# Side work placed head by head in the first pass of an attention and token-mixing kernel

## The chip, the cores and the metric

The kernel runs on one core of a Trainium2 chip. Its time is device microseconds of one execution; a version is run several times and the median counts. A profiled execution gives, beside its own time, a span (from its first to its last instruction) and a record of every engine: TensorE (PE, with its weight loads as PEld), VectorE (DVE), ScalarE (ACT), GpSimd (POOL) and SyncE (SP), which issues nearly all DMAs here from one queue. Each engine works through its own instructions in order.

## The reference

```
h = layernorm(x) * (1 + ca) + sa            # x: 2048 x 1024; the six rows sa ca ga sb cb gb = silu(c) @ w_mod
q, k, v = h @ wq, h @ wk, h @ wv            # 32 heads of 32, four segments of 512 tokens
for s in range(4):                          # per head
    p = softmax(q_s k_s^T * scale + causal mask);  a_dot = p v_s
    a_mem = phi(q_s) M / (phi(q_s) z)       # phi(t) = t + 1 for t > 0, else exp(t)
    out_s = g * a_mem + (1 - g) * a_dot     # g = sigmoid(beta)
    M += phi(k_s)^T v_s;  z += sum phi(k_s)
x = x + ga * (out @ wo)
h = layernorm(x) * (1 + cb) + sb
x = x + gb * mixer(layernorm(h))            # token-mixing MLP: 2048 tokens -> 3584 -> 2048, over 1024 channels
```

All is float32 to the outside. Most matmuls are done as three products of parts: a matrix is split into a high part, rounded to the format that TensorE multiplies at full rate, and the rest ("split": a copy on ScalarE, a subtraction on VectorE or GpSimd).

## The kernel before

There are three stages: a start, in which the first 512 tokens are normalised and modulated (to about 115 us); the attention loop (to about 1080 us); the output projection and the mixer. The change is in the attention loop.

The loop runs over 128 steps n, one per head of an iteration. An iteration t takes one group of four heads and one segment of 512 tokens. The 16 iterations of the first pass cover segments 0 and 1 for the eight groups in turn, the 16 of the second pass segments 2 and 3. So n 0 to 63 is the first pass, n 64 to 127 the second. At step n the loop body writes out, for different heads, the stages of one pipeline: `scores` of head n (L440: score matmuls, exponentials on ScalarE into p, two GpSimd masks at L457, the cast of p to the half-precision ph at L459, the rest of p by two GpSimd subtractions at L461), `maxima` of head n + 3 (L414: matmuls sx, sy, sz and on VectorE the row maxima at L425, which go back into the stacks sk by small DMAs at L437), `values` of head n - 1 (L463: 20 short matmuls pv from ph), and `project` for m = n + 8 (L322: key, value and query matmuls at L185 and L193, and the stacks sk of the head by DMAs L318 to L320).

Beside this main work stands side work:

- Weights of a group. In the first pass `load_part` (L149) loads a raw tile of 512 KB (L154) and splits it into two tiles w at L155 to L158; `keep_w` stores the split weights to DRAM, from where the second pass reloads them. A group has value and key weights in two parts ("v", 0 and 1) and query weights in one ("q").
- Token tiles. `token_tile` (L219) loads 128 tokens of segments 2 and 3 (L222), takes the statistics on VectorE (L128), normalises on ScalarE (L207), transposes on TensorE (L228, tile hpl), modulates on ScalarE (L231), splits (L234, L236) and stores to DRAM (L239). There are eight, at n = 4, 9, ... 39.
- Late modulation. `mod_late` (L498) loads 128 rows of the transposed w_mod (L500) and takes one product with the silu row on VectorE (L501), 32 times, at n = 12, 15, ... 105 (ML0, MLS). After the eighth the rows of ga are written to DRAM, after the last the rest.
- Output weights. `wo_ahead` (L552) loads a piece of wo (L556), multiplies it by ga (tile gaw, GpSimd, L557), splits it (L558, L559) and stores it (L561), eight times, at n = 66, 71, ... 101 (WO0, WOS). `spread` loads gaw at n = 62. The pieces are read back from n = 115 on (wop).

All raw tiles of this side work, the high parts of the token tiles and the wo pieces share one set of three buffers (tag "raw").

The order in which the calls stand is not the order on the engines. A scheduler takes all instructions, by the order of the calls and by when it reckons them ready, and gives each engine its own queue; work that waits for no earlier result, such as a load with a free buffer, can so be pulled far ahead. `tc.issue_after(ins)` adds an edge that keeps what a block contains behind `ins` in the queue of the same engine; it orders issue and waits for nothing.

Of the kernel before, what the change touches and what calls it, by code (L numbers as in the profile page):

```python
# [7 lines left out]
F32 = mybir.dt.float32  # L8
# [26 lines left out]
ML0 = 12  # L35
MLS = 3
HB = 3
WO0 = 66
WOS = 5
# [5 lines left out]
def attention_and_mlp(ctx, tc, x, wq, wkv, wo, beta, w1, b1, w2, b2, c, wm_a, wm_b, out):  # L45
# [26 lines left out]
    acst.tile([P, 24], F32, name="pad2")  # L72
# [75 lines left out]

    def load_part(g, pr, kind, part, res):  # L149


        if pr == 0:
            r = a.tile([P, D], F32, tag="raw", bufs=3, name=f"raw{kind}{g}_{part}")
            SY.dma_start(r, (wkv if kind == "v" else wq)[g, :, 1024 * part:1024 * part + 1024])  # L154
        for i in range(2):  # L155
            w = aw.tile([P, 2, 512], F32R, tag="w", bufs=8, name=f"w{kind}{pr}_{g}_{part}_{i}")
            if pr == 0:
                split(w, r[:, 512 * i:512 * i + 512], A, V)  # L158
            else:
                SY.dma_start(w.bitcast(F32), wsp[g, 2 * part + i if kind == "v" else 4 + i])  # L160
            res[kind, 2 * part + i] = w
# [252 lines left out]
    def maxima(t, h):  # L414
# [8 lines left out]
        for i, o in ((0, x[:, 0:128]), (2, x[:, 128:512]), (1, y[:, 0:256]), (3, z)):  # L423
            T.matmul(o, q[:, 128 * i:128 * i + 128], k[:, 0:128 * i + 128], start=True, stop=True)  # L424
            V.tensor_tensor_reduce(o, o, mask[:, 384 - 128 * i:], 1.0, -3.0e38, op0=ALU.add, op1=ALU.max,  # L425
                                   accum_out=mx[:, h % 2, i:i + 1])
# [12 lines left out]

    def scores(t, h):  # L440
        d = st[t]
        q, k = d["sk", h][:, 0], d["sk", h][:, 1]
# [16 lines left out]
        A.copy(ph[:, 0], p32)  # L459
        for c in (slice(0, 640), slice(640, 1280)):  # L460
            G.tensor_tensor(ph[:, 1, c], p32[:, c], ph[:, 0, c], op=ALU.subtract)  # L461
# [36 lines left out]
    def mod_late(j):  # L498
        r = a.tile([P, D], F32, tag="raw", bufs=3, name=f"rawm{j}")
        SY.dma_start(r, wm_b[P * j:P * j + P])  # L500
        V.scalar_tensor_tensor(r, r, 1.0, scb, op0=ALU.mult, op1=ALU.mult, accum_out=mcol[:, j:j + 1])  # L501
# [50 lines left out]
    def wo_ahead(i):  # L552

        nh, c2 = i // 4, 2 * (i % 4)
        r, hi = (a.tile([P, 2, 512], F32, tag="raw", bufs=3, name=f"wo{n_}{i}") for n_ in ("r", "h"))
        SY.dma_start(r, wo[P * c2:P * c2 + 2 * P, 512 * nh:512 * nh + 512].rearrange("(c p) n -> p c n", p=P))  # L556
        G.tensor_tensor(r, r, gaw[:, 512 * nh:512 * nh + 512].unsqueeze(1).to_broadcast([P, 2, 512]), op=ALU.mult)  # L557
        A.copy(hi.bitcast(F32R), r)  # L558
        V.tensor_tensor(r.bitcast(F32R), r, hi, op=ALU.subtract)  # L559
        for part, t in enumerate((hi, r)):  # L560
            SY.dma_start(wos[c2:c2 + 2, nh, :, part].rearrange("c p n -> p c n"), t)  # L561

    for n in range(-LEADS, 4 * NI + VL):
# [15 lines left out]
        if n == WO0 - 4:  # L579
            spread(gaw, 0)  # L580
        if n >= WO0 and (n - WO0) % WOS == 0 and (n - WO0) // WOS < 8:
            wo_ahead((n - WO0) // WOS)
# [365 lines left out]
```

## Time and profile before

| | |
|---|---|
| median of 3 runs | 2335.71 us (2332.09 to 2339.83) |
| profiled execution, its own time | 2329.09 us |
| span of the profiled execution | 2327.4 us |
| granted TensorE clock, mean over the span | 0.983 |
| chain that ended last, by engine | PE 82%, DMA 6%, DVE 6%, ACT 2%, POOL 2% |
| DMA traffic | 414.67 MB, mean 178 GB/s |

How the views are read: a row of the windows gives, for a stretch of the span, the busy time and the number of instructions of each engine, the clock that TensorE was granted (1.00 is full), the mean busy share of the 16 DMA engines and their rate. A row of the waits gives how long an engine stood idle just before instructions of one line, and what ended the wait. A row of the order of time gives start, duration, engine, line, operation and tiles, with the idle time before it and its releaser in brackets. A row with three durations gives least, median and greatest in ns.

### The profile page before, as it was taken

Reading aid. Unit: us, or ns where it says so; the run is one execution under the profiler, and the core shown is the slowest. Engines: PE = TensorE matmul, PEld = TensorE weight load, DVE = VectorE, ACT = ScalarE, POOL = GpSimd, SP = SyncE. Lnnn points to the kernel's source line nnn. Section 1 sums busy time; section 2 is a strip of 40 time slices with the busy share of each in tenths; the row PEclk is TensorE's granted clock in tenths of the full one; section 3 lists DMA queues with packets and bytes.
Section 4 is the critical chain, followed back from the end, with each engine's and each line's share of the span. In section 5 each row is a group of like instructions: output and inputs, shape, how many; then the busy total and the mean of one; then the engine's idle time right before and its main releaser. Section 6 shows DMA issues by size and latency. Waiting matters only on the chain.

```text
span 2327.4 us, 38419 instructions
## 1 busy us (share of the span) xinstructions
PE 2244.8 (96%) x13866; PEld 1931.2 (83%) x13866; DVE 1693.3 (73%) x3806; ACT 1107.6 (48%) x2010; POOL 721.8 (31%) x827
## 2 busy tenths in 40 slices
PE   8999999999899999998989999999999999999999
PEld 7888888888789999986877888888888788888887
DVE  5666666785776566657889666598889787868687
ACT  5476766655566666655324333353335242424232
POOL 3165555675676555555000000023332000000000
PEclk9999999999999999999999999999999999999999
DMA  6747565788774444374354765465557542423233
GB/s 245 247 122 217 179 185 150 231 295 271 219 218 121 122 119 120 105 238 139 128 195 166 285 227 211 147 251 212 213 213 270 186 136 78 140 69 128 67 116 147
DMA packets 172593, 414.67 MB, mean 178 GB/s; under 512 B 17236, under 2 KB 71540, under 8 KB 163444
## 3 DMA queue, kind: packets, MB, share of 16 engines
q1 hardware_dynamic: 172404, 412.22, 53.3%
q8 instruction: 110, 1.80, 0.3%
q14 instruction: 79, 0.65, 0.1%
HBM read 236.23 MB, written 125.06 MB: 155 GB/s over the span
## 4 chain that ended last, share of the span: by engine, by line
PE 82%; DMA 6%; DVE 6%; ACT 2%; POOL 2%; issue 2%; SPq 1%; DVEq 0%; POOLq 0%; ACTq 0%
PE mx L745 44%; PE nps L185 12%; PE qps L193 7%; PE po L653 6%; PE pv L475 3%; PE sx L424 1%; PE a L446 1%; PE sz L424 1%; DMA rawx<-in_x_dram 1%; DMA rawm<-in_wm_b_dram 1%; PE a L449 1%; DMA wor<-in_wo_dram 1%; PE rd L396 1%; PE a L453 1%; PE up L406 1%
## 5 line engine op out<-in xcount | busy, mean ns | idle before, releaser
L745 PE MATMUL mx<-bU,sp 128*128 128x512 f32 x2352 | 535.6, 389 | 2.6 <-DVE sp L123 1.3
L745 PEld LDWEIGHTS mx<-bU,sp 128*128 128x128 f32 x2352 | 440.9, 188 | 96.8 <-DVE sp L123 2.1
L185 PE MATMUL nps<-wv,h 128*128 128x256 f32 x3072 | 447.6, 287 | 1.3 <-POOL h L123 1.1
L745 PE MATMUL mx<-bA,sp 128*128 128x512 f32 x1764 | 431.7, 389 | 3.4 <-DVE sp L123 1.8
L120 ACT CAST sp<-wr 128x384 fp32r<-128x384 f32 (+2 forms) x408 | 217.3, 545 | 445.5 <-PE mx L745 377.5
L461 POOL TENSOR_TENSOR ph<-p,ph 128x640 f16<-128x640 f32 x256 | 374.5, 1484 | 148.8 <-ACT ph L459 143.4
L185 PEld LDWEIGHTS nps<-wv,h 128*128 128x128 f32 x3072 | 409.8, 192 | 6.3 <-POOL h L123 1.3
L745 PEld LDWEIGHTS mx<-bA,sp 128*128 128x128 f32 x1764 | 330.7, 188 | 73.6 <-DVE sp L123 2.6
L123 DVE TENSOR_TENSOR sp<-wr,sp 128x384 fp32r<-128x384 f32 (+2 forms) x408 | 261.0, 651 | 33.7 <-ACT sp L120 33.2
L752 DVE TENSOR_TENSOR ac<-mx,ac 128x512 f32<-128x512 f32 x280 | 190.4, 689 | 91.0 <-PE mx L745 90.3
L193 PE MATMUL qps<-h,wq 128*128 128x512 f32 x768 | 200.1, 408 | 1.4 <-DVE r L349 1.3
L459 ACT CAST ph<-p 128x1280 f16<-128x1280 f32 x128 | 160.8, 1257 | 69.9 <-POOL p L457 69.3
L653 PE MATMUL po<-wo,ots 128*128 128x512 f32 x768 | 184.0, 398 | 8.1 <-DVE x L656 5.9
L653 PEld LDWEIGHTS po<-wo,ots 128*128 128x128 f32 x768 | 146.5, 192 | 40.1 <-issue 6.7
L193 PEld LDWEIGHTS qps<-h,wq 128*128 128x128 f32 x768 | 147.0, 197 | 31.8 <-issue 1.7
L457 POOL TENSOR_SCALAR_AFFINE_SELECT p<-p 128x256 f32<-128x256 f32 x256 | 126.1, 501 | 138.5 <-ACT p L454 88.4
L475 PE MATMUL pv<-vp,ph 128*128 128x97 bf16 (+1 forms) x2560 | 156.9, 205 | 10.8 <-POOL ph L461 4.5
L425 DVE CUSTOM_DVE_ANT_0 sx<-sx,mask 128x128 f32<-128x128 f32 (+1 forms) x256 | 110.5, 432 | 75.0 <-PE sx L424 73.8
L745 PE MATMUL mx<-bB,sp 128*128 128x512 f32 x588 | 164.5, 389 | 0.0
L475 PEld LDWEIGHTS <-ph 128*128 128x128 f16 x2560 | 121.0, 100 | 40.4 <-issue 17.1
L752 DVE TENSOR_TENSOR cc<-mx,cc 128x512 f32<-128x512 f32 x140 | 94.6, 685 | 53.4 <-PE mx L745 48.4
L745 PEld LDWEIGHTS mx<-bB,sp 128*128 128x128 f32 x588 | 110.3, 188 | 23.3 <-ACT bB L120 0.4
(173 smaller groups left out, 3184.6 us busy)
## 6 DMA issues: line engine op xcount, KB each, us to landing
sk<-sg SPq DMA_DIRECT2D x384, 128.0 KB
wr<-in_w_dram SPq DMA_DIRECT2D x28, 1024.0 KB
wr<-in_w_dram SPq DMA_DIRECT2D x32, 768.0 KB
bstu<-ucd SPq DMA_DIRECT2D x28, 768.0 KB
wsp<-wv SPq DMA_DIRECT2D x32, 512.0 KB
rawm<-in_wm_b_dram SPq DMA_DIRECT2D x32, 512.0 KB
wv<-wsp SPq DMA_DIRECT2D x32, 512.0 KB
pcd<-cc SPq DMA_DIRECT2D x14, 1024.0 KB
```

What stands on the lines that cost most here:

```text
L120: A.copy(hi, src)
L123: lo_eng.tensor_tensor(lo, src, hi.bitcast(F32), op=ALU.subtract)
L185: T.matmul(ps[:, aa], h[:, j, 128 * tt:128 * tt + 128], wt[:, i, o:o + 256], start=(n == 0), stop=(n >= 6 * NK - 2), skip_group_check=True)
L193: T.matmul(ps, wt[:, i, o:o + 128], h[:, j], start=(k + n == 0), stop=(3 * k + n == 3 * NK - 1))
L425: V.tensor_tensor_reduce(o, o, mask[:, 384 - 128 * i:], 1.0, -3.0e38, op0=ALU.add, op1=ALU.max, accum_out=mx[:, h % 2, i:i + 1])
L457: G.affine_select(w, w, pattern=[[0, 2], [1, 128]], compare_op=ALU.is_ge, fill=0.0, base=0, channel_multiplier=-1)
L459: A.copy(ph[:, 0], p32)
L461: G.tensor_tensor(ph[:, 1, c], p32[:, c], ph[:, 0, c], op=ALU.subtract)
L475: T.matmul(pv[:, i, 0:w], ph[:, part, o:o + 128], d["vp"][:, j, h, 0:w], start=(n == 0), stop=(n == 19), skip_group_check=True)
L653: T.matmul(ps, os_[:, i, P * ct:P * ct + P], wop[ct, nh][:, j], start=(n == 0), stop=(n == 3 * NK - 1))
L745: T.matmul(ps, ops[q][:, i, P * k:P * k + P], b[:, j], start=(m == 0 and first), stop=(m == 3 * nk - 1), skip_group_check=True)
L752: V.tensor_tensor(d, ps, d, op=ALU.add)
```

## The change

The calls of the side work are taken out of the loop body and put into a table `todo` by step; each piece of side work is cut into a fetch (its load) and the rest, and the rest is put behind an instruction of that step's own head. `marks` holds, for each step, the last row maximum on VectorE ("V", that of head n + 3), the cast on ScalarE ("A") and the last subtraction on GpSimd ("G").

- Token tiles load into gaw, which is not needed for ga before n = 62, in place of a raw buffer, at n = 0, 5, ... 35, and are worked on two steps later, VectorE's part behind the mark "V".
- The weights of groups 2 to 7 load their parts at steps 0, 1 and 2 after 8g - 13 and are split at steps 1, 3 and 4 after it, ScalarE's part behind the mark "A". Groups 0 and 1 are as before.
- Late modulation j loads at n = 40 + 2j, its product comes at n = 42 + 2j behind the mark "V".
- Output weights i load at n = 65 + 6i, the split comes two steps later, GpSimd's part behind the mark "G"; the piece is multiplied and split in two halves.
- A padding tile is 16 floats smaller, so the mask, the memory, the split weights w and the tiles of the projections and stacks lie 64 bytes lower in each partition. The pages of h, p and ph stay where they were.

```
-ML0 = 12
-MLS = 3
+ML0 = 40
+MLS = 2
-WO0 = 66
-WOS = 5
+WO0 = 65
+WOS = 6
...
-    acst.tile([P, 24], F32, name="pad2")
+    acst.tile([P, 8], F32, name="pad2")
...
+    def fetch_part(g, kind, part):
+        r = a.tile([P, D], F32, tag="raw", bufs=3, name=f"raw{kind}{g}_{part}")
+        SY.dma_start(r, (wkv if kind == "v" else wq)[g, :, 1024 * part:1024 * part + 1024])
+        return r
+
+    def split_part(g, kind, part, r):
+
+        for i in range(2):
+            w = aw.tile([P, 2, 512], F32R, tag="w", bufs=8, name=f"w{kind}0_{g}_{part}_{i}")
+            split(w, r[:, 512 * i:512 * i + 512], A, V)
+            W[0, g][kind, 2 * part + i] = w
...
     def token_tile(tt):
 
-        r = a.tile([P, D], F32, tag="raw", bufs=3, name=f"rawx{tt}")
-        SY.dma_start(r, x[P * tt:P * tt + P])
+        r = gaw
         norm_x(a, r)
...
+    marks = {}
+
+    @contextmanager
+    def behind(n, engines):
+
+        with ExitStack() as s:
+            for e in engines:
+                if (n, e) in marks:
+                    s.enter_context(tc.issue_after(marks[n, e].ins))
+            yield
...
+    def wo_split(i, r):
+
+        nh, c2 = i // 4, 2 * (i % 4)
+        hi = a.tile([P, 2, 512], F32, tag="raw", bufs=3, name=f"woh{i}")
+        for j in range(2):
+            G.tensor_tensor(r[:, j], r[:, j], gaw[:, 512 * nh:512 * nh + 512], op=ALU.mult)
+            A.copy(hi[:, j].bitcast(F32R), r[:, j])
+            V.tensor_tensor(r[:, j].bitcast(F32R), r[:, j], hi[:, j], op=ALU.subtract)
         for part, t in enumerate((hi, r)):
             SY.dma_start(wos[c2:c2 + 2, nh, :, part].rearrange("c p n -> p c n"), t)
+
+    todo = {}
+
+    def plan(n, f, engines=""):
+        todo.setdefault(n, []).append((f, engines))
+
+    def later(n, fetch, m, f, engines):
+
+        got = []
+        plan(n, lambda: got.append(fetch()))
+        plan(m, lambda: f(got[0]), engines)
+
+    for i in range(8):
+        later(5 * i, lambda i=i: SY.dma_start(gaw, x[P * (8 + i):P * (9 + i)]),
+              5 * i + 2, lambda r, i=i: token_tile(8 + i), "V")
+    for g in range(2, NG):
+        n = 8 * g - 13
+        plan(n, lambda g=g: W.__setitem__((0, g), {}))
+        for kind, part, n0, n1 in (("v", 0, 0, 1), ("v", 1, 1, 3), ("q", 0, 2, 4)):
+            later(n + n0, lambda g=g, kind=kind, part=part: fetch_part(g, kind, part),
+                  n + n1, lambda r, g=g, kind=kind, part=part: split_part(g, kind, part, r), "A")
+        plan(n + 4, lambda g=g: keep_w(g))
+    for j in range(32):
+        n = ML0 + MLS * j
+        later(n, lambda j=j: mod_fetch(j), n + 2, lambda r, j=j: mod_late(j, r), "V")
+    plan(WO0 - 3, lambda: spread(gaw, 0))
+    for i in range(8):
+        n = WO0 + WOS * i
+        later(n, lambda i=i: wo_fetch(i), n + 2, lambda r, i=i: wo_split(i, r), "G")
...
-        if 4 <= n < 44 and n % 5 == 4:
-            token_tile(8 + n // 5)
-        if n >= ML0 and (n - ML0) % MLS == 0 and (n - ML0) // MLS < 32:
-            mod_late((n - ML0) // MLS)
+        for f, engines in todo.pop(n, ()):
+            with behind(n, engines):
+                f()
```

More of the change, by code (lines that the diff above doesn't have):

```diff
@@ L1 @@
 import math
-from contextlib import ExitStack
+from contextlib import ExitStack, contextmanager
 import concourse.bass as bass
@@ L147, in attention_and_mlp @@
     raw_w = {}
+    def fetch_part(g, kind, part):
[7 more added lines that the diff above has]
+            W[0, g][kind, 2 * part + i] = w
     def load_part(g, pr, kind, part, res):
         if pr == 0:
-            r = a.tile([P, D], F32, tag="raw", bufs=3, name=f"raw{kind}{g}_{part}")
-            SY.dma_start(r, (wkv if kind == "v" else wq)[g, :, 1024 * part:1024 * part + 1024])
+            split_part(g, kind, part, fetch_part(g, kind, part))
+            return
         for i in range(2):
             w = aw.tile([P, 2, 512], F32R, tag="w", bufs=8, name=f"w{kind}{pr}_{g}_{part}_{i}")
[L157 to L160, printed above, removed]
+            SY.dma_start(w.bitcast(F32), wsp[g, 2 * part + i if kind == "v" else 4 + i])
             res[kind, 2 * part + i] = w
@@ L424, in maxima @@
             T.matmul(o, q[:, 128 * i:128 * i + 128], k[:, 0:128 * i + 128], start=True, stop=True)
-            V.tensor_tensor_reduce(o, o, mask[:, 384 - 128 * i:], 1.0, -3.0e38, op0=ALU.add, op1=ALU.max,
-                                   accum_out=mx[:, h % 2, i:i + 1])
+            marks[4 * t + h - LEADS, "V"] = V.tensor_tensor_reduce(
+                o, o, mask[:, 384 - 128 * i:], 1.0, -3.0e38, op0=ALU.add, op1=ALU.max,
+                accum_out=mx[:, h % 2, i:i + 1])
         if h % 2 == 0:
@@ L578, in attention_and_mlp @@
             reload_h(seg, ct + 1)
[L579 to L582, printed above, removed]
         if 4 * NI - 5 <= m < 4 * NI + 3:
```

17 lines of the change are left out of this document (9 added, 8 removed).

## The prediction

> **What bounds the kernel now.** I read the page first, then a table of three stretches of the attention stage, then the waits of the stretch that turned out to be slow, then the order of time around single stalls. The page says that TensorE is busy nearly all the time:
>
> ```profile
> span 2327.4 us, 38419 instructions
> PE 2244.8 (96%) x13866; PEld 1931.2 (83%) x13866; DVE 1693.3 (73%) x3806; ACT 1107.6 (48%) x2010; POOL 721.8 (31%) x827
> ```
>
> That is an average over stages. The change touches only the loop over the 128 heads (64 of each pass), so I cut that loop by its casts of L459, one for each head. The stretches end where cast 48, cast 72 and cast 112 start; the columns are length, busy time and count of PE, PEld, DVE, ACT, POOL, granted clock, DMA share and rate. The second fence is the same stretches for L459 alone.
>
> ```profile
> core 0: us, PE busy (x) PEld busy (x) DVE busy (x) ACT busy (x) POOL busy (x), PEclk, DMA share, GB/s
> 115.70:492.30 376.60, 354.57 (x2963) 320.07 (x2962) 258.74 (x773) 262.51 (x492) 231.43 (x257) 0.94 0.63 189
> 492.30:693.90 201.60, 185.34 (x1583) 168.60 (x1582) 136.78 (x391) 113.24 (x196) 130.99 (x139) 0.96 0.77 246
> 693.90:975.50 281.60, 280.79 (x2492) 257.98 (x2491) 172.06 (x584) 176.11 (x312) 164.41 (x224) 1.00 0.44 121
> ```
>
> ```profile
> 115.70:492.30 376.60, 60.36 (x48) 0.94 0.63 189
> 492.30:693.90 201.60, 30.21 (x24) 0.96 0.77 246
> 693.90:975.50 281.60, 50.18 (x40) 1.00 0.44 121
> ```
>
> Heads 72 to 111 carry almost no side work. TensorE is never idle there, at full clock: 281.60 / 40 = 7.04 us a head. That is the floor of a head, since an iteration of the first pass does the same matmuls (per two iterations the same reads and updates of the memory). Beside it the first pass has the token tiles' transposes, 0.91 us a tile in the chain that ended last, 8 x 0.91 = 7.3 us:
>
> ```profile
> 219.30 0.91 PE hpl L228 x8
> ```
>
> Heads 0 to 47 take 376.6 - 48 x 7.04 - 7.3 = 31.4 us too long, heads 48 to 71 take 201.6 - 24 x 7.04 = 32.6 us too long: **64 us** that TensorE loses. The same from the other columns: it is idle for 22.0 + 16.3 = 38.3 us, and the clock is 0.06 and 0.04 short, 22.6 + 8.1 = 30.7 us; 69 us less the 7.3 us of transposes is 62. These stretches, and not the 96%, are where side work can win or lose.
>
> Who waits in that stretch (us in total, times, longest):
>
> ```profile
> DVE rawm L501 <- DMA rawm<-in_wm_b_dram: 30.3, 13, 6.8
> ACT wv L120 <- DMA rawv<-in_wkv_dram: 14.4, 6, 5.4
> POOL wor L557 <- DMA wor<-in_wo_dram: 9.4, 4, 5.6
> DVE st L128 <- DMA rawx<-in_x_dram: 3.6, 3, 2.5
> ```
>
> All four are side work at the front of an in-order engine whose load hasn't landed: 57.7 us. How one reaches TensorE:
>
> ```profile
> 626.25 0.58 SPq L500 DMA_DIRECT2D rawm<-in_wm_b_dram  x1
> 631.84 1.23 DVE L501 SCALAR_TENSOR_TENSOR rawm<-rawm,scb 128x1024 f32<-128x1024 f32 x1 [6.79 <-DMA rawm<-in_wm_b_dram]
> 633.80 0.58 PE L424 MATMUL sy<-sk 96*128 96x256 f32 x1 [3.94 <-DVE rdd L398]
> ```
>
> The load is issued at 626.25, VectorE has nothing left that it may do and sits 6.79 us; the row maxima and the memory read stand behind the product, and TensorE runs dry for 3.94 us. The clock then drops. The ten microseconds around this stall and two like it, and the waits at the head of the other two:
>
> ```profile
> 500.00:510.00 10.00, 7.85 (x46) 6.36 (x46) 8.65 (x20) 4.36 (x10) 9.10 (x9) 0.83 0.75 270
> 540.00:550.00 10.00, 7.53 (x55) 7.03 (x54) 6.06 (x20) 5.86 (x11) 5.36 (x3) 0.83 0.96 354
> 630.00:640.00 10.00, 6.20 (x29) 5.25 (x30) 7.53 (x25) 3.54 (x9) 4.42 (x4) 0.66 0.43 160
> ```
>
> ```profile
> 495.13 2.37 POOL L557 TENSOR_TENSOR wor<-wor,gaw 128x1024 f32<-128x1024 f32 x1 [1.64 <-DMA wor<-in_wo_dram]
> 538.89 1.25 DVE L501 SCALAR_TENSOR_TENSOR rawm<-rawm,scb 128x1024 f32<-128x1024 f32 x1 [4.35 <-DMA rawm<-in_wm_b_dram]
> 544.64 2.37 POOL L557 TENSOR_TENSOR wor<-wor,gaw 128x1024 f32<-128x1024 f32 x1 [5.58 <-DMA wor<-in_wo_dram]
> ```
>
> Idle plus missing clock: 2.15 + 1.7, 2.47 + 1.7 and 3.8 + 3.4, together 15.2 us for 1.64 + 4.35 + 5.58 + 6.79 = 18.4 us of waiting, 0.83 us lost for each. Over 57.7 us that makes **48 of the 64 us late loads**; the other 16 I call crowding (0.22 us a head).
>
> The Trainium skill ("TensorE: Matmul & The Clock Gate", Part 1) says that the array falls to half clock after an idle window of about 3.4 us. By that rule only the third of these stalls would have cost clock, and the gain would be the idle part, about 38 us at most; the trace differs, with 0.83 in a stretch whose idle time is 2.15 us in all, so the sum goes by the rows.
>
> **The change part by part.** *Late modulation.* Its 32 products go from every third head from 12 (in the built program of before the scheduler had pulled them as far forward as loads allowed, all done before cast 72) to every second head from 42 to 104, each load two heads ahead and each product behind the row maxima that VectorE then has. The order of the changed program shows exactly that: one product after every second head's maxima, its load on SP at least two heads earlier, 14 us against the 5 to 6 us that passed in the row above. Heads 0 to 41 lose all of it. *Token tiles* (through gaw in place of a raw buffer) load two heads before their statistics; *weights* two heads, in places one, before the splits, which stand behind that head's cast on ScalarE; *wo* pieces load two heads before GpSimd's product, which stands behind that head's subtraction. So the four waits lose their ground. What remains late by a head or less are a few weight loads (the query part of group 6 is issued about one head ahead): I leave 10%, 48 - 5 = 43 us won. Of the crowding in heads 0 to 71 I take half as gone, since the 32 products and all 8 wo pieces are spread over 70 heads in place of some 58: 8 us.
>
> *What comes in.* Durations (ns, min/median/max):
>
> ```profile
> L501 DVE SCALAR_TENSOR_TENSOR rawm<-rawm,scb x32: 1201/1448/3156, 207.6 to 677.5; 128x1024 f32<-128x1024 f32 x32
> L557 POOL TENSOR_TENSOR wor<-wor,gaw x8: 2363/2390/2847, 495.1 to 665.7; 128x1024 f32<-128x1024 f32 x8
> L236 POOL TENSOR_TENSOR rawx<-rawx,hix x16: 1273/1290/2284, 146.0 to 437.5; 128x512 fp32r<-128x512 f32 x16
> L120 ACT CAST wv<-rawv x32: 602/616/645, 16.6 to 460.9; 128x512 fp32r<-128x512 f32 x32
> L123 DVE TENSOR_TENSOR wv<-rawv,wv x32: 661/692/1776, 17.2 to 461.5; 128x512 fp32r<-128x512 f32 x32
> ```
>
> A wo piece in halves costs GpSimd 2 x 1290, ScalarE 2 x 616, VectorE 2 x 692 ns, hence 0.2 us more on GpSimd than one L557 and nothing that TensorE sees. Heads 72 to 111 get 20 products and 7 pieces: VectorE (172.1 + 29.0 + 9.7) / 281.6 = 75%, ScalarE (176.1 + 8.6) / 281.6 = 66%, GpSimd (164.4 + 18.1) / 281.6 = 65%. TensorE stayed full at more than that, in a part of the first pass whose loads were in time:
>
> ```profile
> 270.00:280.00 10.00, 10.00 (x74) 8.45 (x73) 7.77 (x23) 9.50 (x18) 6.26 (x8) 1.00 0.99 336
> ...
> sum 50.00, PE 50.00 PEld 45.76 DVE 38.70 ACT 38.69 POOL 33.33; mean PE 10.00 PEld 9.15 DVE 7.74 ACT 7.74 POOL 6.67
> ```
>
> So this cost lies between 0 and the crowding rate, 41 heads (72 to 112) x 0.22 = 9 us; 50 us are a short witness, I take 9. The pieces' DMAs (each 512 KB in and twice that out, with 512 KB a product) move along and add some 60 GB/s to a stretch at 121. What is late next: the modulation rows for gaw come with product 7 at head 56, and gaw is loaded at 62, six heads or 42 us later; the last wo piece is split behind head 109, the reload begins at 115; the last rows stand at 104, needed after 127. None decides.
>
> *Waits that are added.* The placement orders issues and waits for nothing. But gaw is one buffer, and its next load waits on SP for the store of the tile before; behind it stand that head's stacks (sk). Token tiles are five heads, 35 us, apart, so this is nothing if the tile's chain keeps to its two heads, and otherwise the second rival.
>
> *Weights 64 bytes lower.* No row shows the same matmul at two addresses. The nearest:
>
> ```profile
> L396 PE MATMUL rd<-MZ,pq x192: 273/276/358, 92.2 to 1036.4; 128*128 128x132 f32 x192
> L185 PE MATMUL nps<-wv,h x3072: 276/283/562, 27.0 to 1013.0; 128*128 128x256 f32 x192
> ```
>
> The moving tile of L396 is one of eight that lie 528 bytes apart, so it starts at eight offsets within 128 bytes, and least and median differ by 3 ns. I take nothing; the ends are the 7 ns between the two medians on 3072 matmuls, 21 us either way.
>
> Sum: -43 - 8 + 9 = **-42 us**. The profiled execution took 2329.1 us (span 2327.4), the median of the runs is 2335.7; I take the difference from the median: 2294 us.
>
> **The rivals.**
>
> (a) *The waits move.* The three raw buffers now hold a product's load for over two heads and two buffers of each wo piece, and SP is one queue: a load that waits there for its buffer holds the stacks behind it. For: three buffers for up to four tenants from head 65 on. Against: no piece overlaps in heads 0 to 41, where half of the loss was. Half of the 48 us is won, the 9 paid: -15, 2321 us.
>
> (b) *Slower: the second pass takes the density of heads 48 to 71.* They did 14 products (two instructions each in the row below) and the 8 pieces in 24 heads at 201.6 / 24 = 8.40 us.
>
> ```profile
> 492.30:693.90 201.60, 23.48 (x28) 0.96 0.77 246
> ```
>
> If density sets that pace, and not late loads, heads 72 to 112 pay 41 x 1.36 = 56 us and heads 42 to 71 keep theirs, while heads 0 to 41 win at most 31.4 x 42 / 48 = 27: +29, 2365 us. It turns slower than before from 27 / 41 = 0.66 us a head. Against it: half the density per head, and the 50 us above at full rate. The Trainium skill ("SBUF — State Buffer", Who interferes with whom) speaks for it: a VectorE instruction with two SBUF inputs shuts out a GpSimd instruction that reads SBUF, and the product is one. The trace has products of 1201 to 3156 ns, so something like it is there, though the same 32 ran beside a busier GpSimd before.
>
> (c) *The address decides*: 21 us better, 2273, or worse, 2315.
>
> (d) *It does not do what it says*: TensorE's lost time comes from the chain of each head and not from the loads; the three stalls above speak against it. 2336 us.
>
> **How the numbers follow.** The sum has 0.57 (its own range 2280 to 2310), (a) 0.17, (b) 0.10, (c) 0.06 better and 0.04 worse, (d) 0.06. 0.3%, 7 us, is about what can be told from no change: faster 0.82 (the sum, (c), 0.15 of (a)), within 0.08 ((d) and the rest of (a)), slower 0.10 ((b)). The range 2268 to 2328 takes in both ends of (c), the low end of the sum and (a), and leaves out (b), (d) and a few hundredths below.
>
> **What would show it.** Right: the first 64 casts of L459 take under 475 us in place of 513, the clock in heads 0 to 71 is at least 0.98, the four waits sum to under 12 us, heads 72 to 111 take at most 291 us. Wrong: the waits gone and the pace still over 7.5 us ((d)); waits of SP or of the wo product ((a)); heads 72 to 111 over 300 us with POOL or DVE as TensorE's releaser ((b)); a median of L185 off by 5 ns ((c)).

## The result and the profile after

| | before | after |
|---|---|---|
| median of 4 runs | 2333.90 us (2331.99 to 2339.83) | 2306.51 us (2305.48 to 2307.91) |
| ratio, 95% interval | | 0.988 (0.9865 to 0.9894) |
| profiled execution, its own time | 2329.09 us | 2305.58 us |

The changed kernel is 27 us faster; 42 us were forecast. The first lines of its page:

```profile
span 2303.9 us, 38456 instructions
PE 2232.7 (97%) x13866; PEld 1918.9 (83%) x13866; DVE 1703.9 (74%) x3814; ACT 1105.6 (48%) x2018; POOL 727.9 (32%) x835
```

The cast of each head is L479 now. Cut at the casts of heads 0, 48, 72 and 112, as before:

```profile
core 0: us, PE busy (x) PEld busy (x) DVE busy (x) ACT busy (x) POOL busy (x), PEclk, DMA share, GB/s
112.20:479.90 367.70, 349.86 (x2998) 315.65 (x2997) 250.89 (x742) 262.18 (x494) 222.24 (x258) 0.95 0.60 171
479.90:664.70 184.80, 178.43 (x1541) 162.28 (x1541) 123.33 (x388) 105.99 (x191) 107.20 (x131) 0.97 0.73 227
664.70:952.80 288.10, 280.05 (x2514) 257.74 (x2513) 206.41 (x632) 181.08 (x326) 202.78 (x240) 0.99 0.62 181
```

Heads 0 to 71 take 552.5 us, 25.7 less than before. TensorE's loss there (idle time and missing clock, read off as for before) is 17.8 + 18.4 in the first row and 6.4 + 5.5 in the second: 48 us where it was 69. Heads 72 to 111, which have got the moved work, take 288.1 us, 6.5 more. What lies ahead of the first cast is 3.5 us shorter, what lies behind head 111 0.7 us shorter: together the 23.5 us by which the spans differ.

The same heads cut at head 42 as well, before and then after:

```profile
115.72:454.37 338.65, 319.70 (x2675) 288.31 (x2674) 226.73 (x690) 236.46 (x447) 201.54 (x230) 0.94 0.60 178
454.37:694.02 239.65, 220.31 (x1872) 200.46 (x1872) 168.91 (x475) 139.40 (x242) 160.87 (x166) 0.95 0.79 253
```

```profile
112.18:439.93 327.75, 309.96 (x2612) 278.20 (x2611) 221.53 (x668) 234.41 (x444) 196.63 (x229) 0.95 0.60 173
439.93:664.67 224.74, 218.31 (x1927) 199.71 (x1926) 152.68 (x462) 133.75 (x240) 132.78 (x160) 0.98 0.70 213
```

In these traces the clock is half for whole steps of 3.41 us, and each such step costs 1.71 us. With the steps counted (11 and 7 before, 10 and 3 after) in place of the two-digit mean, TensorE's loss falls from 37.7 to 34.9 us in heads 0 to 41 and from 31.3 to 11.5 us in heads 42 to 71. So nearly all of it was won in heads 42 to 71. The lengths alone say less, since the stretches do not hold quite the same work: 2675 and 1872 matmuls before, 2612 and 1927 after.

The waits in heads 0 to 71, of which the four that summed to 57.7 us were the ground of the forecast:

```profile
SPq L513 <- ACT ot L512: 52.8, 11, 12.7
SPq L604 <- DMA hT<-gaw: 11.5, 5, 4.5
PE kps L363 <- DVE r L356: 6.8, 3, 4.1
PE a L466 <- DMA sk<-nt: 3.2, 2, 1.8
DVE st L128 <- DMA gaw<-in_x_dram: 2.5, 1, 2.5
DVE rawm L524 <- DMA rawm<-in_wm_b_dram: 0.5, 1, 0.5
```

Of the late loads 3.0 us are left: the first step of the forecast came true. But 48 us of TensorE's loss stayed without them, and there are waits that were smaller or absent before: SP behind the stores of a head (L513) and behind the one buffer of the token tiles (L604), and TensorE behind the small copies sk<-nt. The same two rows of SP and TensorE before, the first in heads 0 to 71, the second in heads 0 to 111:

```profile
SPq L493 <- ACT ot L492: 26.8, 8, 10.0
```

```profile
PE a L446 <- DMA sk<-nt: 0.4, 1, 0.4
```

Over heads 0 to 111 the second is 8.2 us after. Two of these stalls in the order of time, the first with the stretch of half clock around it:

```profile
132.44 0.37 SPq L246 DMA_DIRECT2D hT<-gaw  x1
...
135.94 0.35 SPq L604 DMA_DIRECT2D gaw<-in_x_dram  x1
...
141.77 0.69 DVE L128 BATCH_NORM_STATS2 st<-gaw 128x6 f32<-128x512 f32 x1 [2.51 <-DMA gaw<-in_x_dram]
...
143.31 0.90 PE L363 MATMUL kps<-ident,k 128*128 128x128 f32 x3 [4.09 <-DVE r L356]
```

```profile
131.00:148.10 17.10, 11.28 (x48) 8.18 (x47) 10.87 (x30) 11.50 (x20) 12.48 (x16) 0.50 0.66 187
```

The store of one token tile is issued at 132.44; the load of the next into the same buffer goes out at 135.94 only; VectorE stands for 2.51 us at the statistics, and the remainder r, for which TensorE waits, stands behind them. It is the placed work with its load late after all, by the single buffer. The half clock began at 131.03, before this stall, and behind a step of 3.41 us in which TensorE was idle for 0.1 us only; what began it is open. The second, in the second pass:

```profile
779.54 0.58 SPq L520 DMA_DIRECT2D rawm<-in_wm_b_dram  x1
780.16 0.45 SPq L578 DMA_DIRECT2D wor<-in_wo_dram  x1
780.71 0.41 SPq L520 DMA_DIRECT2D rawm<-in_wm_b_dram  x1
781.22 2.63 SPq L445 DMA_DIRECT2D sk<-nt  x4
786.41 0.77 PE L466 MATMUL a<-sk 98*128 98x512 f32 x1 [2.83 <-DMA sk<-nt]
```

Three loads of 512 KB are issued just ahead of the four copies of 2 KB that a head's scores need, and TensorE waits 2.83 us for these.

The other expectations: the first 64 casts take 494.8 us (112.2 to 607.0), not under 475; heads 72 to 111 stay under 291; the clock of heads 0 to 71 is 0.95 and 0.97 in the two rows, not 0.98; the median of the key and value matmuls fell by 5 ns, as in the third rival, and that of the query matmuls rose by 5. The rows of after, and between them the query matmuls of before:

```profile
L193 PE MATMUL nps<-wv,h x3072: 276/278/562, 27.1 to 989.0; 128*128 128x256 f32 x192
```

```profile
L193 PE MATMUL qps<-h,wq x768: 387/389/776, 28.0 to 1021.7; 128*128 128x512 f32 x192
```

```profile
L201 PE MATMUL qps<-h,wq x768: 387/394/776, 28.1 to 996.9; 128*128 128x512 f32 x192
```

### The profile page after: what moved, and what is told of

Its sections match the earlier page's. It is cut to its first block, busy times and chain, and to the rows that moved or that the text cites. A ratio compares the mean times of both kernels' runs of the same rounds, so it can differ in the third digit from the quotient of the medians.

```text
span 2303.9 us, 38456 instructions
## 1 busy us (share of the span) xinstructions
PE 2232.7 (97%) x13866; PEld 1918.9 (83%) x13866; DVE 1703.9 (74%) x3814; ACT 1105.6 (48%) x2018; POOL 727.9 (32%) x835
## 4 chain that ended last, share of the span: by engine, by line
PE 81%; DVE 9%; DMA 5%; ACT 2%; issue 1%; POOL 1%; SPq 0%; DVEq 0%; ACTq 0%
PE mx L798 41%; PE nps L193 14%; PE qps L201 7%; PE po L706 6%; PE pv L495 3%; DMA wr<-in_w_dram 1%; PE a L466 1%; PE sx L431 1%; DVE ac L805 1%; PE sz L431 1%; DVE bU L123 1%; PE rd L403 1%; DVE sp L123 1%; DMA sk<-nt 1%; PE a L469 1%
## 5 line engine op out<-in xcount | busy, mean ns | idle before, releaser
L193 PE MATMUL nps<-wv,h 128*128 128x256 f32 x3072 | 438.2, 284 | 0.7 <-DVE sg L123 0.5
L481 POOL TENSOR_TENSOR ph<-p,ph 128x640 f16<-128x640 f32 x256 | 379.6, 1504 | 159.0 <-ACT ph L479 153.5
L193 PEld LDWEIGHTS nps<-wv,h 128*128 128x128 f32 x3072 | 403.8, 190 | 6.8 <-DVE sg L123 0.7
L123 DVE TENSOR_TENSOR sp<-wr,sp 128x384 fp32r<-128x384 f32 (+2 forms) x408 | 256.8, 641 | 29.4 <-ACT sp L120 29.2
L479 ACT CAST ph<-p 128x1280 f16<-128x1280 f32 x128 | 160.8, 1257 | 41.1 <-POOL p L477 40.3
L477 POOL TENSOR_SCALAR_AFFINE_SELECT p<-p 128x256 f32<-128x256 f32 x256 | 120.5, 480 | 129.2 <-ACT p L470 63.4
L495 PE MATMUL pv<-vp,ph 128*128 128x97 bf16 (+1 forms) x2560 | 146.6, 204 | 5.5 <-DVE mv L134 2.7
L495 PEld LDWEIGHTS <-ph 128*128 128x128 f16 x2560 | 117.5, 100 | 29.4 <-issue 12.1
```

What stands on the lines that cost most here:

```text
L123: lo_eng.tensor_tensor(lo, src, hi.bitcast(F32), op=ALU.subtract)
L193: T.matmul(ps[:, aa], h[:, j, 128 * tt:128 * tt + 128], wt[:, i, o:o + 256], start=(n == 0), stop=(n >= 6 * NK - 2), skip_group_check=True)
L477: G.affine_select(w, w, pattern=[[0, 2], [1, 128]], compare_op=ALU.is_ge, fill=0.0, base=0, channel_multiplier=-1)
L479: marks[n, "A"] = A.copy(ph[:, 0], p32)
L481: marks[n, "G"] = G.tensor_tensor(ph[:, 1, c], p32[:, c], ph[:, 0, c], op=ALU.subtract)
L495: T.matmul(pv[:, i, 0:w], ph[:, part, o:o + 128], d["vp"][:, j, h, 0:w], start=(n == 0), stop=(n == 19), skip_group_check=True)
```

## The experiments

Three questions: what the address is worth, what of the placement carries the gain, and what holds the 48 us that stayed. The table collects all kernels. The stretches are cut at the casts of heads 0, 42, 72 and 112 in each profiled execution; "behind" is from the cast of head 112 to the end of the span; "ratio" is that to runs of the kernel before taken beside the kernel, with its 95% interval, so it need not be the quotient of the medians shown. In brackets stands TensorE's loss in the stretch: its idle time, and 1.71 us for each step of 3.41 us at half clock.

| kernel | median us | ratio | heads 0-41 | 42-71 | 72-111 | behind |
|---|---|---|---|---|---|---|
| before | 2333.90 | | 338.7 (37.7) | 239.7 (31.3) | 281.6 (0.8) | 1351.8 |
| after | 2306.51 | 0.988 (0.9865 to 0.9894) | 327.8 (34.9) | 224.7 (11.5) | 288.1 (9.8) | 1351.1 |
| addr_only | 2329.87 | 0.9983 (0.9969 to 0.9996) | 337.8 (39.0) | 240.1 (33.1) | 279.3 (0.4) | 1355.0 |
| place_only | 2308.62 | 0.9891 (0.9873 to 0.9909) | 326.7 (34.0) | 227.0 (9.6) | 290.8 (10.3) | 1348.8 |
| addr_plus64 | 2309.78 | 0.9893 (0.9876 to 0.9911) | 327.9 (34.4) | 225.0 (8.5) | 290.0 (9.9) | 1350.7 |
| no_pin | 2342.89 | 1.0038 (1.002 to 1.0056) | 335.0 (44.9) | 240.6 (28.6) | 289.9 (12.4) | 1359.9 |
| early_modulation | 2325.55 | 0.9966 (0.9952 to 0.998) | 346.6 (51.9) | 217.3 (9.9) | 289.9 (9.0) | 1357.9 |
| early_no_loads | 2296.43 | 0.9824 (0.9797 to 0.9851) | 320.2 (29.4) | 217.8 (4.9) | 285.4 (6.5) | 1358.5 |
| early_no_products | 2294.94 | 0.9824 (0.9805 to 0.9844) | 332.1 (35.4) | 221.3 (9.0) | 277.2 (0.5) | 1349.9 |
| late_no_products | 2307.69 | 0.9882 (0.9856 to 0.9909) | 332.1 (40.5) | 221.0 (9.9) | 286.7 (5.1) | 1353.2 |
| no_tile_work | 2283.22 | 0.979 (0.9772 to 0.9808) | 302.9 (20.5) | 227.7 (17.0) | 286.1 (10.2) | 1347.0 |
| bulk_on_scalar | 2313.25 | 0.9918 (0.9902 to 0.9934) | 332.8 (41.1) | 227.7 (12.0) | 288.5 (9.1) | 1346.3 |
| fetch_behind_copies | 2320.83 | 0.9956 (0.9941 to 0.9971) | 317.4 (22.7) | 230.7 (21.1) | 296.8 (10.4) | 1354.8 |
| early_fetch_behind | 2306.95 | 0.987 (0.9844 to 0.9895) | 323.7 (27.0) | 220.4 (9.9) | 295.9 (15.3) | 1354.9 |

**The yardstick.** Kernels that differ by the address alone have the same order on the engines; their stretches, and the losses in them, agree within some 3 us (before and addr_only; after, place_only and addr_plus64). An edit of anything else makes the scheduler order the whole loop anew: between after and early_fetch_behind, whose calls for heads 72 to 111 are the same, the sequence of VectorE's instructions in that stretch agrees by 54%, and the stretch takes 295.9 us in place of 288.1. So a difference below some 8 us in one stretch may be the new order and not the edit.

### The address

In the kernel before, addr_only lowers the padding tile alone:

```
-    acst.tile([P, 24], F32, name="pad2")
+    acst.tile([P, 8], F32, name="pad2")
```

> The kernel before with the padding tile alone cut from 24 to 8 floats: same instructions in the same order, and the weights, stacks and projection tiles lie 64 bytes lower. Theory P (the gain is placement, the address is worth nothing, as the prediction took it): within 3 us of the kernel before, ratio 0.999 to 1.001, the median of the key and value matmuls stays at 283 ns. Theory A (the address carries part of it): that median falls to 278 ns as in the changed kernel and the query matmuls go from 389 to 394; 3072 x 5 ns less 768 x 5 ns is 11.5 us, so about 10 to 15 us less than before, ratio 0.9935 to 0.996.

place_only is the changed kernel with 24 there, addr_plus64 with 40.

> The changed kernel with the padding tile back at 24 floats: its order on every engine, the addresses of before. Theory P: the whole gain stays, ratio to before 0.987 to 0.990 (about 27 us). Theory A: the medians are back at 283 and 389 ns and 11 to 15 us of the 27 are lost, ratio 0.993 to 0.9955 (12 to 16 us).

> The changed kernel with the padding tile at 40 floats: its order, the same tiles 64 bytes higher than before in place of 64 lower. If what counts is where the weights lie within 128 bytes relative to the pages of h (theory A, by place), this is the changed kernel again: median 278 ns, ratio to before 0.986 to 0.990. If a particular address counts (a row of memory, a neighbour), or nothing does (theory P), the median is 283 and the ratio that of place_only under A, or that of the changed kernel under P with 283 ns.

In the kernel before, the lower address alone wins 4 us (0.9983, 0.9969 to 0.9996). In the changed kernel no gain is clear of the noise: 2306.51 with it, 2308.62 without, 2309.78 at 64 bytes higher, and the three intervals overlap. The median of the key and value matmuls is 278 ns with it, in both kernels, and 283 without; at 64 bytes higher it is 279, and that kernel is no faster than the one with 283. So 3072 x 5 ns = 15 us less 768 x 5 ns = 4 us, some 11 us on paper, were worth 4 in the one kernel, and in the other nothing that shows. The placement carries the gain: with the old address, place_only is 25 us faster than the runs of before beside it.

### What of the placement

no_pin leaves every piece in its step, but without the edges behind that step's row maximum, cast or subtraction:

```
-                if (n, e) in marks:
+                if False:
```

> The changed kernel without the edges that hold a piece behind its head's own work: the fetches two heads ahead, the steps and the cut of the wo pieces stay, the scheduler may pull the rest of a piece ahead of its head's work as soon as its load allows. If the early fetch is what removes the waits for loads, the time stays within 5 us of the changed kernel (ratio to before 0.986 to 0.991). If the pin does it, the waits of in-order engines for rawm, rawv and wor come back (over 20 us in the first 72 heads) and 10 us or more are lost (ratio 0.992 or more).

2342.89 us, 9 slower than before, and a good half of the waits is back, here in heads 0 to 71:

```profile
DVE rawm L524 <- DMA rawm<-in_wm_b_dram: 13.2, 7, 4.4
ACT wv L120 <- DMA rawv<-in_wkv_dram: 11.5, 4, 4.0
ACT wq L120 <- DMA rawq<-in_wq_dram: 4.3, 2, 3.7
DVE st L128 <- DMA gaw<-in_x_dram: 3.0, 1, 3.0
```

Later steps in the program and loads two heads ahead gain nothing by themselves: without the edges the scheduler pulls the pieces forward again, up to their loads; the products run from 415.7 to 726.5 us, where the changed kernel has them from 426.6 to 894.2. The edge is what makes the step hold.

Two things in the stretches qualify this. What no_pin loses against before lies behind head 71 (8.3 us in heads 72 to 111, 8.1 behind them); heads 0 to 71 are 2.8 us shorter than before. And against the changed kernel these heads are 23.1 us longer for 30.4 us more of waits for loads (1.4 us of GpSimd for wo included), 0.76 us for each, close to the forecast's rate. But the pieces stand elsewhere too: heads 42 to 71 have 22 of the 32 products, where the changed kernel has 15, and five of the eight wo pieces, where it has one. So this does not price the lateness alone.

early_modulation keeps placement and edges, and puts the modulation back near its old steps:

```
-ML0 = 40
-MLS = 2
+ML0 = 10
+MLS = 3
```

> The changed kernel with its modulation placed in the same way but from step 10, every third step, close to where it stood before. Theory of the placement (loads in time are what counts): it costs little, 2300 to 2315. Theory of the spread (heads 0 to 41 win because the modulation has left them): heads 0 to 42 go back to before's 338.7 us or more, heads 72 to 112 return to 281.6, net 2312 to 2330.

This run decided most. Its loads are in time: in heads 0 to 71 VectorE waits 4.0 us for rawm and 1.8 for the token tiles, and ScalarE and GpSimd not at all for loads. By the forecast's rate of 0.83 that is worth 43 us. The kernel is 8 us faster than before. Heads 42 to 71, where the three stalls of the forecast stood, are 22.4 us shorter, with a loss of 9.9 us where it was 31.3. But heads 0 to 41, where a third of its pieces stand, are 8 us *longer*, or at the best no shorter (a loss of 51.9 us where it was 37.7), and heads 72 to 111 are 8.3 us longer. So the rule of the late loads fails in heads 0 to 41. From 2325.6 to 2306.5, the step of 19 us, heads 0 to 41 give 18.8 (346.6 to 327.8), because the modulation has left them; the other stretches change by +7.4, -1.8 and -6.8 us, which nearly cancel. What the product does there with its load landed:

```profile
439.80 0.45 DVE L432 CUSTOM_DVE_ANT_0 sy<-sy,mask 128x256 f32<-128x256 f32 x1
440.18 0.13 DVE L432 DVE_READ_ACCUMULATOR2_ANT mx<- 128x1 f32 x1
440.60 1.46 DVE L524 SCALAR_TENSOR_TENSOR rawm<-rawm,scb 128x1024 f32<-128x1024 f32 x1 [0.29 <-DMA rawm<-in_wm_b_dram]
...
442.08 0.53 DVE L432 CUSTOM_DVE_ANT_0 sx<-sx,mask 128x384 f32<-128x384 f32 x1
...
442.72 0.47 PE L431 MATMUL sx<-sk 96*128 96x128 f32 x1 [1.38 <-DVE mx L432]
```

The wait is 0.29 us; the 1.46 us of the product themselves stand between two row maxima, and TensorE runs dry for 1.38 us.

Is it the products or their loads? early_no_loads takes the loads out of early_modulation, early_no_products cuts the products to 8 columns, late_no_products does the latter in the changed kernel:

```
-        SY.dma_start(r, wm_b[P * j:P * j + P])
...
-        V.scalar_tensor_tensor(r, r, 1.0, scb, op0=ALU.mult, ...)
+        V.scalar_tensor_tensor(r, scb, 1.0, scb, op0=ALU.mult, ...)
```

```
-        V.scalar_tensor_tensor(r, r, 1.0, scb, op0=ALU.mult, ...)
+        V.scalar_tensor_tensor(r[:, 0:8], r[:, 0:8], 1.0, scb[:, 0:8], op0=ALU.mult, ...)
```

> The kernel with its modulation placed from step 10, every third step (2325.6 us; heads 0 to 42 346.5 us against 327.8 in the changed kernel), with the 32 loads of the modulation rows left out; each product is taken of the silu row with itself, so the modulation rows are wrong. If the loads (512 KB each in SP's queue and on the DMA engines) are what costs heads 0 to 42 their 18.7 us, these fall to 327 to 333 and the time to 2306 to 2313. If it is VectorE's 1.25 us each, nothing moves: 2321 to 2328.

> The same kernel (modulation from step 10, every third step) with all its loads, but each product cut to its first 8 columns, so the modulation rows are wrong. The mirror of the run without loads: if VectorE's time is the cost, heads 0 to 42 fall to 327 to 333 us and the time to 2306 to 2313; if the loads are, nothing moves: 2321 to 2328. If both runs win half, each piece costs by both.

> The changed kernel with all its loads, but each product of the modulation cut to its first 8 columns, so the modulation rows are wrong. With the modulation placed from step 10 the same cut was worth 31 us (2325.6 to 2294.9). If the place decides what a product costs, the cut is worth little here: the 9 us that I put down for the second pass or less, 2297 to 2305, with heads 72 to 112 falling from 288.2 to 280 to 285. If a product costs the same wherever it stands, the cut is worth some 30 us again: 2272 to 2282.

Either cut is worth as much as all of the gain, 29 and 31 us, more than the half that was put down for this case: a piece costs by its load and by its product, and the two do not add up, as if with one of them gone the other found room. In heads 0 to 41, which hold 11 of the 32 pieces, the loads are worth 26.4 us and the products 14.5, both beyond the yardstick. The same cut of the products where the changed kernel has them is worth nothing (2307.69 against 2306.51; no stretch moves by more than 4.3 us, though TensorE's loss in heads 72 to 111 falls from 9.8 to 5.1). VectorE's row says that the cut itself took hold: 148 ns at least and 434 at the median, where the whole product takes 1208 and 1270 in after:

```profile
L524 DVE SCALAR_TENSOR_TENSOR rawm<-rawm,scb x32: 148/434/1165, 429.6 to 897.1; 128x8 f32<-128x8 f32 x32
```

So what a product costs depends on where it stands. How the 31 us of the early cut are spread over the stretches is less certain: heads 72 to 111 fall by 12.7 us in it, with fewer products there than the changed kernel has, and that is of the order of the reshuffling.

### What holds heads 0 to 41

no_tile_work leaves out the work of the token tiles but keeps their traffic:

```
     def token_tile(tt):
-        r = gaw
-        norm_x(a, r)
...
+        r = hi = gaw
```

> The changed kernel without the work of the eight token tiles: their load into gaw and two stores stay, the statistics, normalisation, transposes, modulation and split of segments 2 and 3 are left out. If heads 0 to 41 are held by the tiles' work and by its single buffer, heads 0 to 42 fall from 327.8 us to near the floor of 42 x 7.04 = 296, some 25 to 32 us less, 7.3 of it the transposes: 2274 to 2282. If the weight splits and the loads of that part are what crowds, only the transposes and little more go: 8 to 14 us, 2292 to 2298.

```profile
119.62:422.50 302.88, 290.91 (x2550) 263.64 (x2549) 211.82 (x606) 193.04 (x348) 178.75 (x213) 0.97 0.56 159
```

Heads 0 to 41 fall by 24.9 us to 302.9, 7 us above 42 x 7.04 = 295.7. So 7.3 us of what they take too long are the transposes, and some 17 us are the tiles' other work: statistics, normalisation and split between the head's own pieces. TensorE's loss there says somewhat less, 34.9 to 20.5, hence 14 us. Which of these pieces costs it was not tried, and the edit also frees a raw buffer (that of the tiles' high parts). Heads 42 to 71 come as near to the forecast's floor in early_modulation, with 217.3 beside 30 x 7.04 = 211.2.

### SP's queue

bulk_on_scalar issues the loads of the modulation and of the wo pieces from ScalarE's own queue:

```
-        SY.dma_start(r, wm_b[P * j:P * j + P])
+        A.dma_start(r, wm_b[P * j:P * j + P])
...
-        SY.dma_start(r, wo[P * c2:P * c2 + 2 * P, ...
+        A.dma_start(r, wo[P * c2:P * c2 + 2 * P, ...
```

> The changed kernel, with the loads of the modulation rows (rawm) and of the wo pieces (wor) issued from ScalarE's own DMA queue in place of SP's. Queue theory (what is left of the loss is the small copies sk<-nt and the stores behind 512 KB loads in SP's one queue): the waits of PE's scores on sk<-nt go, stretches 48 to 64 and 72 to 96 lose most of their 12.3 us of idle time and their clock loss, the time falls by 6 to 15 us to 2292 to 2300, ratio 0.982 to 0.986. Rival, crowding (the side pieces themselves stand between a head's own pieces on VectorE and GpSimd): idle time and time as in the changed kernel, 2306 within 4, ratio 0.988. Third: the transfers share the same DMA engines whatever queue issues them, so the small copies stay as slow, also 2306, and ScalarE's issue time adds up to 5 us.

The queue theory falls. The copies were indeed held by the bulk loads ahead of them, since TensorE's wait for sk<-nt goes from 8.2 to 1.5 us; but the time is 2313 us, and other waits have grown. TensorE's own, in heads 0 to 111 of this kernel and then of after:

```profile
PE kps L363 <- DVE r L356: 8.8, 6, 4.4
PE sx L431 <- DVE mx L432: 4.3, 7, 1.4
PE sy L431 <- DVE mx L432: 4.1, 7, 1.4
...
PE sz L431 <- DVE mx L432: 3.1, 4, 1.2
...
PE a L466 <- DMA sk<-nt: 1.5, 3, 1.0
```

```profile
PE a L466 <- DMA sk<-nt: 8.2, 4, 2.8
PE kps L363 <- DVE r L356: 7.4, 4, 4.1
...
PE sx L431 <- DVE mx L432: 2.4, 5, 0.6
PE sz L431 <- DVE mx L432: 2.4, 4, 1.2
PE sy L431 <- DVE mx L432: 1.8, 4, 1.1
```

The three waits for the row maxima grow from 6.6 to 11.5 us. In heads 42 to 111 alone, which hold the moved loads, the wait for sk<-nt falls by 6.7 us, those for the row maxima grow by 3.7, and those for ScalarE's exponentials from 1.8 to 3.5. These heads take 516.2 us where they took 512.8, so other waits took the place of the one that went. Heads 0 to 41, where only two of the moved loads stand, are 5.0 us longer; that may be the new order.

fetch_behind_copies keeps one queue and holds every fetch behind that step's copies; early_fetch_behind does so for the token tiles and weights alone:

```
-                SY.dma_start(sk[96 + part:97 + part, 0]...
+                last = SY.dma_start(sk[96 + part:97 + part, 0]...
+        for m in (0, 1):
+            marks[4 * t + h - LEADS + m, "S"] = last
...
-        plan(n, lambda: got.append(fetch()))
+        plan(n, lambda: got.append(fetch()), "S")
```

> The changed kernel, with every fetch of the side work held on SP behind that step's last small copy sk<-nt. Queue theory: the small copies no longer stand behind a bulk load issued just before, waits on sk<-nt go, 2294 to 2302, ratio 0.983 to 0.987. If it is the DMA engines that are shared and not the order of issue, a bulk load issued behind the copies slows the next step's copies instead: 2306 within 4. Slower (to 2320) if the fetches now come so late that products and splits wait again: waits of VectorE on rawm or ScalarE on wv over 10 us.

> The changed kernel, with only the loads of the token tiles and of the weights held behind that step's small copies sk<-nt; loads of the modulation and of the wo pieces stay where the changed kernel has them. With all fetches held, heads 0 to 42 took 317.4 us (changed kernel 327.8) and heads 42 to 112 lost 14.5 us to late loads of rawm. If the two parts are separate, this one keeps the first and not the second: 2306 - 10 = 2296, range 2290 to 2301, waits of VectorE on rawm under 3 us, faster than the changed kernel. If the gain of heads 0 to 42 came from an accident of the order, it stays at 2306 within 4.

With all fetches held, heads 0 to 41 take 317.4 us, 10 less than in the changed kernel, but the loads of the modulation come late again, and the time is 2320.83:

```profile
DVE rawm L526 <- DMA rawm<-in_wm_b_dram: 43.6, 19, 4.7
```

Here 43.6 us of late loads, three quarters of the 57.7 before, cost heads 42 to 111 only 14.7 us (527.5 against 512.8), 0.34 us for each and not 0.83; even that holds the reshuffling. The kernel that keeps only the early part has 323.7 us in heads 0 to 41, wins 4.3 us in heads 42 to 71 and loses 7.8 in heads 72 to 111, whose calls it doesn't touch. It ends where the changed kernel does (0.987, 0.9844 to 0.9895, beside 0.988, 0.9865 to 0.9894). No complete kernel of this study was shown faster than the changed one.

## Why the prediction was right in direction and too large

The direction, the likeliest case and its own range held: 2306.5 lies in 2280 to 2310, 12.5 us above the forecast. Term by term, in the profiled executions:

- *Late loads, -43.* The mechanism is right as far as the waits go: 57.7 us before, 3.0 after, where 10% had been left standing. Its size is wrong. The step that failed is "0.83 us lost for each. Over 57.7 us that makes 48 of the 64 us late loads". The rate came from three stalls, chosen because a stall of TensorE stood behind each and all of them in heads 42 to 71, and was laid on all 26 waits. In heads 42 to 71 it nearly came: 28.0 us of these waits went to 0.5 and TensorE's loss from 31.3 to 11.5, 0.72 us for each, though seven wo pieces and six products left these heads as well, and no run tells the two apart. In heads 0 to 41 it did not: 29.7 us went to 2.5 and the loss from 37.7 to 34.9, 0.10 us for each, though ten of the eleven products left them as well. Other kernels give other rates (0.76 in no_pin, 0.34 in fetch_behind_copies), with other orders. What decides whether TensorE runs dry behind a late load was not isolated.
- *Crowding, -8.* The 16 us that were left over after the late loads were taken as the whole of it, and no row priced it. Where the runs price it, it is larger: the tiles' other work costs heads 0 to 41 some 14 to 17 us, and the modulation's pieces cost them 18.8 (early_modulation against after; 17.0 by TensorE's loss), with 4.0 us of late loads among them at most. But little of that was won against before, since early_modulation, with the same eleven products in these heads and the late loads nearly gone, loses 14.2 us more there than the kernel before. So something else in the changed kernel cost heads 0 to 41 about what the spread of the modulation won; whether that is the token tiles' single buffer, the edges or merely the new order is open. Both terms together were -51; measured are 48 - 69 = -21 us of TensorE's loss in heads 0 to 71, and -25.7 us of time (the clock's two digits leave some 3 us open in each of the losses).
- *Second pass, +9.* The size came, and that is luck: addr_only and after have the same address, and heads 72 to 111 differ by 288.1 - 279.3 = +8.8 us. But the reason given, a crowding rate per head, is not what was found there: the products, 16 in the trace and not the 20 of the working, are worth 1.4 us (288.1 to 286.7), and 5.0 of TensorE's 8.1 us of idle time are two waits for the copies sk<-nt (2.21 and 2.83 us). Which part of the rest is loads and which wo pieces was not tried.
- *The address, 0.* The ends were 21 us either way; 4 us were measured in the kernel before, and nothing clear of the noise in the changed one. The median did move by the 5 ns named as the sign of the third rival, and for little time: "a median of L185 off by 5 ns" was no test of what the matmul is worth on the path.
- *Waits that are added, nothing.* It was put at nothing "if the tile's chain keeps to its two heads", and the chain doesn't always. SP waited 11.5 us for the store of the tile before, and behind one of these waits stands TensorE's longest stall in heads 0 to 111, 4.09 us. What it costs in all wasn't isolated: no run gave the tile a second buffer.
- *Of the rivals,* (a) named what came (waits of SP, with the copies of a head behind them) at 2321 us; the raw buffers, where it looked for them, were not the place. (b) fell: heads 72 to 111 stay at 288.1 us, with VectorE busy for 206.4 / 288.1 = 72%. The Trainium skill ("SBUF — State Buffer", Who interferes with whom), which spoke for it, may hold for single instructions, since the product still takes 1208 to 2372 ns in after; cutting the products was worth no time there. (d) is half right, and its sign came: the waits are gone and the pace of heads 0 to 71 is 552.5 / 72 = 7.67 us, over 7.5. What holds heads 0 to 41 is in good part side work between the pieces of a head's own chain.
- *The cross-check.* The working compared its 64 us with 69 us of idle time and missing clock less 7.3 us for the transposes. But transposes are matmuls and count as busy, so nothing is to be taken off: 69 stands beside 64.

The stall behind the three loads at 779.54 us was foreseen by no step. The fetches were planned for three successive steps (n = 40 + 2j beside n = 65 + 6i), but a fetch has no edge, and the scheduler was free to put one right behind the other in SP's queue, ahead of copies that a head waits for. The working followed when a load is issued and when it is needed, not what stands behind it.

## What to carry to other kernels

A wait for a late load is worth what TensorE loses behind it, not its own length: count the stalls of the engine that bounds, stretch by stretch, and ask of each wait whether that engine ran dry behind it. A rate read in one stretch need not hold in the next (0.72 and 0.10 us here). To learn what side work costs, cut it to a few columns where it stands; the same products were worth 31 us in all at one place and nothing at another. And an edit that lets a scheduler order a loop anew moves stretches that it doesn't touch (8 us here), so compare against kernels that keep the order, and pin a piece whose place matters: the placement without its edges was slower than the kernel before.

## What the runs showed of the hardware

The clock falls after quite short stalls of TensorE, but not after every one. Behind a stall of 1.85 us (ended at 523.3), one of 1.81 us (at 556.4), one of 2.21 us (at 702.5) and the one of 2.83 us at 786.4, all of them in after:

```profile
523.56:526.97 3.41, 3.41 (x14) 3.12 (x14) 1.50 (x6) 1.75 (x3) 1.63 (x3) 0.50 0.95 347
557.70:564.52 6.82, 6.12 (x29) 5.37 (x29) 4.35 (x14) 3.52 (x6) 5.44 (x5) 0.50 0.39 123
702.55:709.38 6.83, 6.83 (x36) 5.56 (x37) 2.77 (x10) 2.38 (x5) 1.26 (x3) 1.00 0.50 169
786.41:789.80 3.39, 3.39 (x26) 2.90 (x27) 0.59 (x2) 2.52 (x4) 0.61 (x1) 0.50 0.00 0
```

The third column from the end is the granted clock: 0.50 for one or two steps of 3.41 us after three of them, 1.00 after the third in time, though it is the second longest. The Trainium skill ("TensorE: Matmul & The Clock Gate", Part 1) has a window of that length that runs freely; the steps agree, while its "after ≥1 idle window (~3.4µs)" would need 3.4 us of idleness and these rows show half clock after 1.8 us.

The stall of 2.21 us differs from the others in where it lies. Cut on from the half-clock rows in steps of 3.41 us, the other three stalls fall into one step each (520.15:523.56, 554.29:557.70 and 782.98:786.39, with TensorE idle for 1.85, 1.81 and 2.81 us), while it is split between two (697.64:701.05 and 701.05:704.46, idle for 0.72 and 1.49 us). Over the 16 steps at full clock of before and after, from 60 us to 1100 us, in which TensorE was idle for 1.8 us or more, half clock followed every time. Below 1.7 us both came: full clock behind 1.65 us in before, half behind 0.11 us in after. So the idle time of a step is not the whole rule, and the rest of it is open.

A shift of 64 bytes in the partitions, with everything else alike, changes the spacing of matmuls: 283 to 278 ns at the median for key and value matmuls (weights from the shifted tile, moving data from pages that stayed), 389 to 394 for the query matmuls, where the two change roles. At 64 bytes higher instead it is 279 for the key and value matmuls.
